# Filling the token slots from two tiles with dump numbers, four tiles for the quarter sums, three tiles for r, a fourth of the squares on ScalarE

## The chip, the cores and the metric

One core of a Trainium2 chip runs the whole program in one launch. The metric is device time in microseconds (us), the median of three runs; lower is better. The engines are TensorE (PE, with its weight loads as PEld), VectorE (DVE), ScalarE (ACT), GpSimd (POOL) and SyncE (SP). Transfers are issued from two queues here, SP's (hardware descriptors, q1 in the views) and POOL's (software descriptors, q0), and are carried by the same 16 DMA engines.

## The reference

```python
scores = matmul(z, z.T) / S                  # 4 batches, S = 3072, z has 64 columns
out = matmul(maximum(scores, 0) ** 2, v)     # v: 3072 x 256
x = (u * out).reshape(12288, 256)

e_idx = argmax(x @ w_gate)                   # 8 experts, top one
for e in range(8):
    h = maximum(x[mask] @ w1[e], 0)          # 256 -> 1024 -> 256
    y[mask] = gate * eom * (h @ w2[e])

h = maximum(y @ w_in, 0)                     # 256 -> 1024, halves u and v
v_n = layer norm of v
v_s = einsum('ts,bsd->btd', w_spatial, v_n) + b_spatial
result = (u * v_s) @ w_out
```

## The kernel before

Every product is made of three matmuls of high and low parts (float32r), so each operand is split into `hi` on ACT and `lo` on DVE. PE, ACT, DVE and SP run in the order in which the code issues; POOL's order is chosen by the framework's scheduler, from what each instruction waits for.

The program has four stages: attention with routing (0 to about 1120 us), the experts (to about 1760), the hidden layer and the norm (to about 2120), and the spatial product, made with two levels of Strassen sums.

**Attention** runs over 576 steps: 4 batches b, 6 column blocks j of 512, 24 row blocks k of 128. For every fourth step PE makes the scores of four steps (L270, 12 matmuls); each step then has `relu` (L218, ACT, tile `r`), `hi` = square of r (L276, ACT), `a` = the same square in full precision (L279 on ACT where `i % 3 == 1`, else L281 on DVE), `lo = a - hi` (L283, DVE), and six matmuls with v (`pv`, L228 to L230), four steps later. `r` has four tiles, shared by all steps. A **group** below is four steps.

Three queues of generators are pumped in the loop. `back` holds the preparation of z and v (load on SP, splits on ACT and DVE, three raw tiles). `fore` holds `route`: after each j it takes 512 tokens through the gates and issues four indirect DMAs on POOL (L429) that scatter their rows, with token number and gate, to a slot in `x_slots`. `slow` holds `first_sums`: 36 times it loads two tiles `sw` of the spatial weight on SP (L788), makes four sums on DVE (L792, L794, L797, L800) and stores each from POOL (L793, L795, L798, L801) to `w_parts`. `sw` has two tiles, and a group of sums uses both, so the next load on SP waits for the stores; whatever SP has behind it (u, z, v loads) waits as well.

The slots must hold something where no token lands. `fill_slots` writes zeros to them in three parts of eight transfers, from one tile of 290 columns that is read again and again (L159), and the parts are queued at steps 22, 46 and 70; each part and each scatter write `x_slots` and wait for each other. `route` drains the current part before it scatters.

**Experts**: `moe_x` loads and turns a chunk of slots and makes, with four small DVE operations (L598 to L601), the row to which each slot's result goes: the token, or for an empty slot a dump row of its own, computed from the tables `marks` and the expert's fill count.

Of the kernel before, what the change touches and what calls it, by code (L numbers as in the profile page):

```python
# [27 lines left out]
F32 = mybir.dt.float32  # L28
F32R = mybir.dt.float32r
BF16 = mybir.dt.bfloat16  # L30
I32 = mybir.dt.int32
AF = mybir.ActivationFunctionType
ALU = mybir.AluOpType
AX = mybir.AxisListType

P = 128
B, S, D, DQK = 4, 3072, 256, 64
N = B * S
E, F = 8, 1024
# [17 lines left out]
class _Kernel:  # L57
# [58 lines left out]
    def setup(self):  # L116
        self.low = [self.below.tile([P, 1024], F32R, name=f"G{i}") for i in range(16)]
        self.G = deque(self.low[0:12])
        self.Z = deque(self.kept[0:6] + self.low[12:])
        self.Z.extend(self.big.tile([P, 1024], F32R, name=f"Z{i}") for i in range(2))  # L120
        nc, wk = self.nc, self.wk
        self.tri = self.pe.tile([P, P], BF16, name="tri", bufs=1)
        make_upper_triangular(nc, self.tri, val=1.0, diag=False)
        self.ones = self.pe.tile([P, P], BF16, name="ones", bufs=1)
        nc.gpsimd.memset(self.ones, 1.0)
        self.WG = self.pe.tile([P, 2, XD], F32R, name="WG", bufs=1)
        self.desc = wk.tile([P, E], F32, name="desc", bufs=1)
        self.base = wk.tile([P, 5, E], F32, name="base", bufs=1)
        for e in range(E):
            nc.gpsimd.memset(self.desc[:, e : e + 1], float(E - e))  # L130
            nc.gpsimd.memset(self.base[:, 0, e : e + 1], float(e * REG))
        self.zeros = self.big.tile([P, W], F32, name="zeros", bufs=1)
        nc.gpsimd.memset(self.zeros, 0.0)
        marks = wk.tile([P, 2, E, CAP // P], I32, name="marks", bufs=1)
        for r0, nt in self.CHUNKS:
            for n, (first, step) in enumerate(((0, REG), (N, CAP))):
                part = marks[:, n, :, r0 : r0 + nt]
                nc.gpsimd.iota(part, pattern=[[step, E], [1, nt]], base=first + r0 * P, channel_multiplier=nt)
        self.marks = wk.tile([P, 2, E, CAP // P], F32, name="marksf", bufs=1)
        nc.vector.tensor_copy(self.marks, marks)  # L140
        self.tokid = wk.tile([P, NT], I32, name="tokid", bufs=1)
        nc.gpsimd.iota(self.tokid, pattern=[[P, NT]], base=0, channel_multiplier=1)

# [7 lines left out]
            nc.vector.tensor_copy(g[:, 0:16], wraw[:, c])  # L151
            nc.vector.tensor_tensor(g[:, 16:32], wraw[:, c], _f(g[:, 0:16]), op=ALU.subtract)

    def fill_slots(self, q):
        r0 = 4 * q
        nt = 4 if q < 2 else CAP // P - r0
        for e in range(E):
            dst = self.xs[e * REG + r0 * P : e * REG + (r0 + nt) * P, :].rearrange("(p r) d -> p r d", p=P)
            self.nc.gpsimd.dma_start(dst, self.zeros.unsqueeze(1).to_broadcast([P, nt, W]))  # L159
            yield  # L160

    def z_prep(self, b, c, dst):
        nc = self.nc
# [33 lines left out]
    def attention(self):  # L197
# [8 lines left out]
        self.drain(deque([zg[0], vg[0]]))  # L206
        self.gate_weights()
        self.back.extend([vg[1], zg[1], vg[2], vg[3], zg[2], vg[4], vg[5]])
        fill = self.fill = deque()

        LAG = 4
        score = [*bank[0:3], bank[7]]
# [1 line left out]
        hl, rs, uts = {}, {}, {}  # L214

        def relu(i):
            rs[i] = self.big.tile([P, 512], F32, name="r", bufs=4)
            nc.scalar.activation(rs[i], score[i % 4], AF.Relu, scale=1.0 / S)  # L218

        def pv(i):  # L220
# [26 lines left out]
        for i, (b, j, k) in enumerate(steps):  # L247
            if i == 0:
                load_u(0)
            if i == NK:  # L250
                self.slow.append(self.first_sums())
            if k == 8:
                load_u(i // NK + 1)
            if k == 0:
                if j == 2 and b + 1 < B:
                    self.back.extend([self.z_prep(b + 1, c, z[b + 1]) for c in range(3)])
                if j == 2 and b == B - 1:
                    self.w0 = []
                    self.back.append(self.w_prep(0, self.w0))
            if k % 4 == 0:  # L260
                self.until(z[b], j // 2)
                self.until(z[b], k // 8)
                (QH, QL), (KH, KL) = z[b][j // 2], z[b][k // 8]
                cs = slice((j % 2) * 512, (j % 2) * 512 + 512)
                for m in (0, 2):
                    for n, (w, x) in enumerate(((KH, QH), (KL, QH), (KH, QL))):
                        for t in range(2):
                            ck = slice((k % 8 + m + t) * P, (k % 8 + m + t) * P + P)
                            rows = slice(64 * t, 64 * t + 64)
                            nc.tensor.matmul(score[m + t], w[rows, ck], x[rows, cs], start=(n == 0), stop=(n == 2))  # L270
                relu(i)
            if k % 4 < 3:
                relu(i + 1)
            r = rs.pop(i)
            hi = self.pe.tile([P, 512], F32R, name="hi", tag="t2h", bufs=6)
            nc.scalar.activation(hi, r, AF.Square)  # L276
            a = self.big.tile([P, 512], F32, name="a", bufs=3)
            if i % 3 == 1:
                nc.scalar.activation(a, r, AF.Square)  # L279
            else:  # L280
                nc.vector.tensor_tensor(a, r, r, op=ALU.mult)  # L281
            lo = self.pe.tile([P, 512], F32R, name="lo", tag="t2l", bufs=5)
            nc.vector.tensor_tensor(lo, a, _f(hi), op=ALU.subtract)  # L283
            hl[i] = (hi, lo)
            if i >= LAG:
                pv(i - LAG)
            self.pump(self.fore)
            if b == B - 1 and j == NJ - 1:
                self.pump(self.fore)
                if k == 12:  # L290
                    self.first_chunk()
            self.pump(self.back)
            if i < NK:
                self.pump(self.back)
            if i < 3 * NK and k == 22:
                fill.append(self.fill_slots(i // NK))
            if i % 2 == 0:
                self.pump(fill)
            if i >= NK and i % 2 == 0 and (j in (1, 3, 4) or b and (j == 0 and k >= 8 or j == 2 and (k >= 12 or b == B - 1))):
                self.pump(self.slow)  # L300
            if j == NJ - 1 and k == NK - 1:
                for t in z.pop(b).values():
                    self.Z.extend(t)
# [6 lines left out]
    def first_chunk(self):  # L310
        nc = self.nc
        self.drain(self.fore)
        self.early = self.wk.tile([P, 1], F32, name="early", bufs=1)
        nc.vector.tensor_copy(self.early, self.base[:, 0, 0:1])
        nc.vector.tensor_scalar(self.base[:, 0, 0:1], self.base[:, 0, 0:1], 1024.0, None, op0=ALU.max)
        self.rows0 = {c: self.moe_load(0, c * 512, 4) for c in range(2)}
        self.x0 = []
        held = [self.G.popleft() for _ in range(2)]
        self.low = [t for t in self.low if all(t is not h for h in held)] + held

        def later():
            for _ in range(13):
                yield
            yield from self.moe_x(self.rows0.pop(0), 0, 0, 4, self.x0, self.early, held, self.bank[3:5])

        self.fore.append(later())

    def route(self, b, j, acc, ut):
# [93 lines left out]
        tt(rk, rk, oh, op=ALU.mult)  # L422
        sl = m4("sl")
        red(sl, rk, AX.X, ALU.add)
        self.drain(self.fill)
        slot = m4("slot", I32)
        nc.vector.tensor_copy(slot, sl)
        for i in range(4):
# [135 lines left out]
        self.nc.sync.dma_start(rows[:, 0:nt, :], src.rearrange("(p r) d -> p r d", p=P))  # L564
        return rows

    def moe_x(self, rows, e, r0, nt, dst, end=None, into=None, T=None):
        nc, wk = self.nc, self.wk
        end = self.base[:, 0, e : e + 1] if end is None else end
        xh, xl = into or (self.e4(F32R), self.e4(F32R))  # L570
        n = nt * P
        T = T or self.bank[6:8]
# [20 lines left out]
        low(1)  # L593
        ids = wk.tile([P, 4], I32, name="ids", bufs=3)
        gate = wk.tile([P, 4], F32, name="gate", bufs=3)
        own, spare = (self.marks[:, k, e, r0 // P : r0 // P + nt] for k in range(2))
        t = wk.tile([P, 4], F32, name="idt", bufs=2)[:, 0:nt]
        nc.vector.tensor_copy(t, rows.bitcast(I32)[:, 0:nt, ID])  # L598
        nc.vector.tensor_tensor(t, t, spare, op=ALU.subtract)
        nc.vector.scalar_tensor_tensor(t, own, end, t, op0=ALU.is_lt, op1=ALU.mult)  # L600
        nc.vector.tensor_tensor(ids[:, 0:nt], t, spare, op=ALU.add)  # L601
        nc.vector.tensor_copy(gate[:, 0:nt], rows[:, 0:nt, ID + 1])
        dst.append((xh, xl, ids, gate))

# [66 lines left out]
    def moe(self):  # L671
# [41 lines left out]
        for i, (c, f) in enumerate(seq):  # L713
# [13 lines left out]
                    self.slow.append(self.gmlp_weights())  # L727
            if f == 3 and c + 1 < len(chunks):
                xx[c + 1] = []
                self.fore.append(self.moe_x(rows.pop(c + 1), *chunks[c + 1], xx[c + 1], self.early if c == 0 else None))  # L730
            if c == 0 and f == 7:
                self.drain(self.fore)
            if f == (5 if c else 7) and c + 2 < len(chunks):
# [47 lines left out]
    def first_sums(self):  # L781

        nc, tt = self.nc, self.nc.vector.tensor_tensor
        for n, (r, c) in self.QUARTER.items():
            for tb, k in [(tb, k) for tb in range(2) for k in range(6)]:
                g = [self.big.tile([P, 768], F32, name="sw", bufs=2) for _ in range(2)]
                for th in range(2):
                    nc.sync.dma_start(g[th].rearrange("p (s t) -> p s t", s=2), self.wsq[r, c, 2 * th + tb, k])  # L788
                yield
# [621 lines left out]
```

## Time and profile before

| | |
|---|---|
| median of three runs | 3420.19 us (3416.14 to 3421.24) |
| profiled execution | 3423.64 us |
| its span, first to last instruction | 3421.8 us |
| PE busy | 3361.7 us |
| DVE busy | 2606.0 us |
| ACT busy | 1678.8 us |
| POOL busy | 717.5 us |

Times in the views are counted from the start of the span. PE is the engine to watch: nearly all its time is matmuls, so a microsecond in which it waits in the first stage is a microsecond of the whole. Busy time of the other engines lies beside it.

### The profile page before, as it was taken

To read this page: it belongs to the slowest core of one execution; us is meant where nothing else is said; L and a number is where in the kernel's file an instruction comes from. 1 tells how busy PE (TensorE), PEld (TensorE's weight loads), DVE (VectorE), ACT (ScalarE), POOL (GpSimd) and SP (SyncE) were. 2 spreads that over 40 slices of the span, in tenths; PEclk is the share of its full clock that TensorE was granted. 3 is DMA by queue.
4 is the path that set the end of the run, shared out by engine and by line. 5 is a ranking of instruction groups with operands and counts; after the bars stand their busy time and mean duration, and the time that the engine had idled before them with its cause. 6 is when DMAs were issued, how large, how long until landed. Compare 5 with 4: busy or idle time off the path is not lost.

```text
span 3421.8 us, 51102 instructions
## 1 busy us (share of the span) xinstructions
PE 3361.7 (98%) x18192; PEld 2970.3 (87%) x18192; DVE 2606.0 (76%) x4803; ACT 1678.8 (49%) x3142; POOL 717.5 (21%) x1037
## 2 busy tenths in 40 slices
PE   7989999999999999999999999999999999999999
PEld 5767777777777888888888889999999999999999
DVE  6768788787887688977768887576767777777777
ACT  6757767677767433333334453333333343343432
POOL 1211121221121356665543320000000000100000
PEclk9999999999999999999999999999999999999999
DMA  5453332323340477777748887576767586975854
GB/s 146 143 149 96 101 115 87 108 96 105 106 137 30 151 263 267 270 275 266 247 156 292 299 317 270 186 263 225 274 219 272 188 282 208 263 264 190 285 195 164
DMA packets 269292, 681.73 MB, mean 199 GB/s; under 512 B 30128, under 2 KB 117952, under 8 KB 269024
## 3 DMA queue, kind: packets, MB, share of 16 engines
q1 hardware_dynamic: 186144, 409.89, 36.5%
q0 software_dynamic: 82880, 268.46, 22.4%
q8 instruction: 144, 2.36, 0.3%
q14 instruction: 124, 1.02, 0.1%
HBM read 429.38 MB, written 248.85 MB: 198 GB/s over the span
## 4 chain that ended last, share of the span: by engine, by line
PE 86%; DVE 5%; DMA 4%; issue 3%; POOL 1%; ACT 1%; DVEq 0%; SPq 0%; POOLq 0%; ACTq 0%
PE bank L1209 11%; PE bank L1208 11%; PE bank L1210 11%; PE bank L228 8%; PE bank L229 7%; PE bank L230 7%; PE bank L270 6%; PE bank L690 4%; PE bank L751 2%; PE bank L752 2%; PE bank L753 2%; PE bank L691 2%; PE bank L975 1%; PE bank L974 1%; PE bank L973 1%
## 5 line engine op out<-in xcount | busy, mean ns | idle before, releaser
L283 DVE TENSOR_TENSOR lo<-a,hi 128x512 fp32r<-128x512 f32 x576 | 394.5, 691 | 156.4 <-ACT a L279 93.0
L218 ACT ACTIVATE r<-bank 128x512 f32<-128x512 f32 x576 | 330.1, 599 | 299.9 <-PE bank L270 272.6
L228 PE MATMUL bank<-hi,G 128*128 128x512 f32 x1152 | 469.1, 407 | 0.0
L229 PE MATMUL bank<-lo,G 128*128 128x512 f32 x1152 | 452.3, 393 | 10.6 <-DVE lo L283 10.6
L1322 ACT ACTIVATE wh<-raw 128x768 fp32r<-128x768 f32 x294 | 247.9, 845 | 417.0 <-PE bank L1210 320.7
L230 PE MATMUL bank<-hi,G 128*128 128x512 f32 x1152 | 450.2, 391 | 0.0
L1208 PE MATMUL bank<-wh,R 128*128 128x384 f32 x1288 | 430.3, 334 | 0.7 <-ACT os L1100 0.7
L1209 PE MATMUL bank<-wl,R 128*128 128x384 f32 x1288 | 430.3, 334 | 0.1
L1210 PE MATMUL bank<-wh,R 128*128 128x384 f32 x1288 | 430.2, 334 | 0.0
L1323 DVE TENSOR_TENSOR wl<-raw,wh 128x768 fp32r<-128x768 f32 x294 | 280.4, 954 | 195.3 <-ACT wh L1322 194.6
L276 ACT ACTIVATE hi<-r 128x512 fp32r<-128x512 f32 x576 | 361.0, 640 | 0.0
L1208 PE MATMUL bank<-wh,K 128*128 128x384 f32 x1064 | 356.8, 335 | 3.9 <-ACT os L1100 3.9
L1209 PE MATMUL bank<-wl,K 128*128 128x384 f32 x1064 | 356.5, 335 | 0.0
L1210 PE MATMUL bank<-wh,K 128*128 128x384 f32 x1064 | 356.4, 335 | 0.0
L755 ACT ACTIVATE hh<-bank 128x512 fp32r<-128x512 f32 (+2 forms) x256 | 132.8, 519 | 386.7 <-PE bank L753 341.6
L228 PEld LDWEIGHTS bank<-hi,G 128*128 128x128 f32 x1152 | 217.4, 189 | 92.0 <-issue 52.0
L281 DVE TENSOR_TENSOR a<-r 128x512 f32<-128x512 f32 x384 | 262.4, 683 | 31.4 <-ACT r L218 30.4
L690 PE MATMUL bank<-G,hh 128*128 128x512 f32 x728 | 263.7, 395 | 0.0
L229 PEld LDWEIGHTS bank<-lo,G 128*128 128x128 f32 x1152 | 218.0, 189 | 50.0 <-DVE lo L283 11.4
L230 PEld LDWEIGHTS bank<-hi,G 128*128 128x128 f32 x1152 | 217.6, 189 | 47.1
L1208 PEld LDWEIGHTS bank<-wh,R 128*128 128x128 f32 x1288 | 241.8, 188 | 1.1 <-ACT os L1100 1.0
L1209 PEld LDWEIGHTS bank<-wl,R 128*128 128x128 f32 x1288 | 241.8, 188 | 0.5 <-DVE wl L1323 0.4
(279 smaller groups left out, 7388.3 us busy)
## 6 DMA issues: line engine op xcount, KB each, us to landing
raw<-w_parts SPq DMA_DIRECT2D x240, 384.0 KB
ra<-v_ops SPq DMA_DIRECT2D x147, 512.0 KB
v_ops<-vu POOLq DMA_DIRECT2D x84, 512.0 KB
xi<-partial SPq DMA_DIRECT2D x48, 768.0 KB
sw<-wsq SPq DMA_DIRECT2D x72, 384.0 KB
w_parts<-sw POOLq DMA_DIRECT2D x144, 192.0 KB
u_hid<-vu POOLq DMA_DIRECT2D x48, 512.0 KB
us<-u_hid SPq DMA_DIRECT2D x31, 768.0 KB
```

The source lines that it names most:

```text
L218: nc.scalar.activation(rs[i], score[i % 4], AF.Relu, scale=1.0 / S)
L228: nc.tensor.matmul(acc[d], vh[:, c], hi, start=(k == 0), stop=False)
L229: nc.tensor.matmul(acc[d], vh[:, c], lo, start=False, stop=False)
L230: nc.tensor.matmul(acc[d], vl[:, c], hi, start=False, stop=(k == NK - 1))
L276: nc.scalar.activation(hi, r, AF.Square)
L281: nc.vector.tensor_tensor(a, r, r, op=ALU.mult)
L283: nc.vector.tensor_tensor(lo, a, _f(hi), op=ALU.subtract)
L690: nc.tensor.matmul(acc, hh[:, tc_], w, start=(f == 0), stop=False)
L1208: nc.tensor.matmul(ps, vh, wh[:, ws], start=(k == 0), stop=False)
L1209: nc.tensor.matmul(ps, vh, wl[:, ws], start=False, stop=False)
L1210: nc.tensor.matmul(ps, vl, wh[:, ws], start=False, stop=(k == 5))
L1323: tt(lo, raw, _f(hi), op=ALU.subtract)
```

## The change

- `fill_slots` is one generator of 32 transfers. It has two tiles `fz` of four rows of 290 columns, cleared once; before each transfer an iota on POOL writes the dump numbers of that chunk into the ID column of one of them, and the transfer copies that tile. The generator stands first in `slow` and is pumped twice a step in the first 24 steps.
- An empty slot then carries its dump row's number, so `moe_x` only converts the ID column; `marks`, `zeros`, `early` and three of its small operations go.
- `first_sums` has four tiles `sw`; it is no longer pumped in the first half of j = 2 of the last batch.
- `r` has three tiles, in the `work` pool under the tag `t2r`, which `f64_prep` uses later.
- `a` is squared on ACT where `i % 4 == 1` (144 of 576 steps; 192 before).

```diff
-        self.zeros = self.big.tile([P, W], F32, name="zeros", bufs=1)
-        nc.gpsimd.memset(self.zeros, 0.0)
...
-    def fill_slots(self, q):
-        r0 = 4 * q
-        nt = 4 if q < 2 else CAP // P - r0
+    def fill_slots(self):
+        nc = self.nc
+        fz = [self.big.tile([P, 4, W], F32, name=f"fz{i}") for i in range(2)]
+        for t in fz:
+            nc.gpsimd.memset(t, 0.0)
+        i = 0
         for e in range(E):
-            dst = self.xs[e * REG + r0 * P : e * REG + (r0 + nt) * P, :].rearrange("(p r) d -> p r d", p=P)
-            self.nc.gpsimd.dma_start(dst, self.zeros.unsqueeze(1).to_broadcast([P, nt, W]))
-            yield
+            for r0, nt in self.CHUNKS:
+                t = fz[i % 2][:, 0:nt, :]
+                i += 1
+                nc.gpsimd.iota(t.bitcast(I32)[:, :, ID], pattern=[[1, nt]], base=N + e * CAP + r0 * P, channel_multiplier=nt)
+                dst = self.xs[e * REG + r0 * P : e * REG + (r0 + nt) * P, :]
+                nc.gpsimd.dma_start(dst.rearrange("(p r) d -> p r d", p=P), t)
+                yield
...
-        fill = self.fill = deque()
+        self.slow.append(self.fill_slots())
...
-            rs[i] = self.big.tile([P, 512], F32, name="r", bufs=4)
+            rs[i] = wk.tile([P, 512], F32, name="r", tag="t2r", bufs=3)
...
-            if i % 3 == 1:
+            if i % 4 == 1:
                 nc.scalar.activation(a, r, AF.Square)
...
-            if i < 3 * NK and k == 22:
-                fill.append(self.fill_slots(i // NK))
-            if i % 2 == 0:
-                self.pump(fill)
-            if i >= NK and i % 2 == 0 and (j in (1, 3, 4) or b and (j == 0 and k >= 8 or j == 2 and (k >= 12 or b == B - 1))):
+                self.pump(self.slow)
+                self.pump(self.slow)
+            elif i % 2 == 0 and (j in (1, 3, 4) or b and (j == 0 and k >= 8 or j == 2 and k >= 12)):
                 self.pump(self.slow)
...
-        self.drain(self.fill)
...
-        own, spare = (self.marks[:, k, e, r0 // P : r0 // P + nt] for k in range(2))
-        t = wk.tile([P, 4], F32, name="idt", bufs=2)[:, 0:nt]
-        nc.vector.tensor_copy(t, rows.bitcast(I32)[:, 0:nt, ID])
-        nc.vector.tensor_tensor(t, t, spare, op=ALU.subtract)
-        nc.vector.scalar_tensor_tensor(t, own, end, t, op0=ALU.is_lt, op1=ALU.mult)
-        nc.vector.tensor_tensor(ids[:, 0:nt], t, spare, op=ALU.add)
+        nc.vector.tensor_copy(ids[:, 0:nt], rows.bitcast(I32)[:, 0:nt, ID])
...
-                g = [self.big.tile([P, 768], F32, name="sw", bufs=2) for _ in range(2)]
+                g = [self.big.tile([P, 768], F32, name="sw", bufs=4) for _ in range(2)]
```

Where the instructions stand now. On POOL at the program's start, before (wraw holds the gate weights):

```order
L133 MEMSET zeros 128x290
L138 IOTA marks 128x8x4 x4
L138 IOTA marks 128x8x3 x2
L138 IOTA marks 128x8x2 x2
L142 IOTA tokid 128x96
L147 DMA wraw<-wg 128x2x16
L159 DMA x_slots<-zeros 512x1x290 x8
L675 IOTA lim 128x4
L793 DMA w_parts<-sw 128x384
```

And of the change, at the same place:

```order
L133 IOTA tokid 128x96
L138 DMA wraw<-wg 128x2x16
L149 MEMSET fz_211 128x1160
L149 MEMSET fz_212 128x1160
L155 IOTA fz_211 128x4
L662 IOTA lim 128x4
L155 IOTA fz_212 128x4
L157 DMA x_slots<-fz_211 128x1160
L157 DMA x_slots<-fz_212 128x1160
L155 IOTA fz_211 128x3
L157 DMA x_slots<-fz_211 128x870
```

Eight transfers in a row, which wait for no buffer, have become two; every later one stands behind an iota that waits until its tile's last transfer has landed. This goes on for 32 transfers, with two stores of sums just ahead of the last; then come the stores of the sums.

On POOL around the second scatter (the second of the program's 24), before:

```order
L429 DMA x_slots<-rows,slot 99328x290 x4
L159 DMA x_slots<-zeros 640x1x290 x2
L793 DMA w_parts<-sw 128x384
L795 DMA w_parts<-sw 128x384
L159 DMA x_slots<-zeros 640x1x290
L798 DMA w_parts<-sw 128x384
L159 DMA x_slots<-zeros 640x1x290 x2
L801 DMA w_parts<-sw 128x384
L159 DMA x_slots<-zeros 640x1x290 x3
```

And of the change (its first row is the first and the second scatter):

```order
L422 DMA x_slots<-rows,slot 99328x290 x8
L780 DMA w_parts<-sw 128x384
L782 DMA w_parts<-sw 128x384
L785 DMA w_parts<-sw 128x384
L788 DMA w_parts<-sw 128x384
```

The fills that stood among the stores of the third group of sums, and those between the two scatters, have left.

On ACT, one group during the same `route` (e is xh of the tokens), before:

```order
L218 ACTIVATE r<-bank_66 128x512
L218 ACTIVATE r<-bank_67 128x512
L276 ACTIVATE hi<-r 128x512
L279 ACTIVATE a<-r 128x512
L218 ACTIVATE r<-bank_68 128x512
L276 ACTIVATE hi<-r 128x512
L340 ACTIVATE e_1738<-e_1737 128x512
L218 ACTIVATE r<-bank_73 128x512
```

And of the change:

```order
L216 ACTIVATE r<-bank_66 128x512
L216 ACTIVATE r<-bank_67 128x512
L274 ACTIVATE hi<-r 128x512
L216 ACTIVATE r<-bank_68 128x512
L274 ACTIVATE hi<-r 128x512
L277 ACTIVATE a<-r 128x512
L334 ACTIVATE e_1774<-e_1773 128x512
L216 ACTIVATE r<-bank_73 128x512
```

The square on ACT has moved from a group's first step to its second, where it stands in every group now; before, its place went round. PE's order has not changed at all, and SP's only in that two of the last loads of `sw` stand behind one more load of u.

## Rows read from the trace of the kernel before

**Rows 1.** The page: busy time, share of the span and instructions of each engine.
```profile
PE 3361.7 (98%) x18192; PEld 2970.3 (87%) x18192; DVE 2606.0 (76%) x4803; ACT 1678.8 (49%) x3142; POOL 717.5 (21%) x1037
```

**Rows 2.** Waits of PE, 36 to 1118 us: us in total, times, longest.
```profile
PE bank L229 <- DVE lo L283: 10.6, 2, 10.1
```

**Rows 3.** Chain that ended last, 0 to 1400 us: start, us, what.
```profile
104.97 1.58 PE bank L270 x12
...
150.36 1.58 PE bank L270 x12
...
253.49 1.58 PE bank L270 x12
...
436.58 1.58 PE bank L270 x12
...
709.77 1.58 PE bank L270 x12
...
987.07 1.58 PE bank L270 x12
```

**Rows 4.** The same chain, 156 to 200 us.
```profile
161.03 2.86 DMA x_slots<-rows,slot
...
170.02 15.24 DMA w_parts<-sw
```

**Rows 5.** Timelines of DVE and ACT near 195, 955 and 410 us; idle before in brackets.
```profile
194.79 0.56 DVE L792 TENSOR_TENSOR sw<-sw 128x384 f32<-128x384 f32 x1 [16.87 <-DMA sw<-wsq]
...
955.23 0.56 DVE L792 TENSOR_TENSOR sw<-sw 128x384 f32<-128x384 f32 x1 [5.01 <-DMA sw<-wsq]
...
410.40 0.63 ACT L180 ACTIVATE K<-raw 128x512 fp32r<-128x512 f32 x1 [3.15 <-DMA raw<-z]
```

**Rows 6.** Waits of SP's queue, 0 to 420 us.
```profile
SPq L788 <- DMA w_parts<-sw: 233.7, 29, 49.6
```

**Rows 7.** Timeline of all engines, 0 to 45 us, and of POOL near 111.
```profile
4.71 5.23 POOL L159 DMA_DIRECT2D x_slots<-zeros  x7
...
26.83 0.63 ACT L180 ACTIVATE G<-raw 128x512 fp32r<-128x512 f32 x1 [8.12 <-DMA raw<-v]
...
28.00 2.13 PE L270 MATMUL bank<-K,K 64*128 64x512 f32 x6 [6.02 <-ACT r L218]
...
34.32 1.15 ACT L180 ACTIVATE G<-raw 128x512 fp32r<-128x512 f32 x2 [3.32 <-DMA raw<-v]
...
36.00 1.64 PE L270 MATMUL bank<-K,K 64*128 64x512 f32 x5 [4.68 <-ACT r L218]
...
110.90 1.46 POOL L429 DMA_INDIRECT x_slots<-rows,slot  x1 [3.54 <-ACT hi L276]
```

**Rows 8.** DMA queues, 10 to 28 us, 34 to 43, 10 to 43: packets, MB, share.
```profile
q0 software_dynamic: 985, 4.07, 81.9%
q1 hardware_dynamic: 899, 1.24, 24.4%
...
q1 hardware_dynamic: 1529, 2.24, 71.2%
...
q1 hardware_dynamic: 2969, 4.43, 43.4%
```

**Rows 9.** Groups of instructions by line, 0 to 1500 us.
```profile
L283 DVE TENSOR_TENSOR lo<-a,hi 128x512 fp32r<-128x512 f32 x576 | 394.5, 691 | 156.4 <-ACT a L279 93.0 <-ACT hi L276 17.2 <-issue 1.5
...
L218 ACT ACTIVATE r<-bank 128x512 f32<-128x512 f32 x576 | 330.1, 599 | 299.9 <-PE bank L270 272.6 <-issue 15.7 <-DVE a L281 11.6
L281 DVE TENSOR_TENSOR a<-r 128x512 f32<-128x512 f32 x384 | 262.4, 683 | 31.4 <-ACT r L218 30.4 <-issue 1.0
```

**Rows 10.** Busy time by windows: us, then PE, PEld, DVE, ACT, POOL, clock, DMA.
```profile
571.24:616.63 45.39, 45.39 (x236) 34.75 (x235) 38.68 (x82) 35.79 (x74) 7.47 (x8) 1.00 0.22 72
```

**Rows 11.** Groups of DVE, 1118 to 1810 us; waits of PE, 1118 to 1300.
```profile
L600 DVE SCALAR_TENSOR_TENSOR idt<-marksf,base,idt 128x4 f32<-128x4 f32 x14 | 3.1, 223 | 0.5
...
PE bank L751 <- DVE hlo L757: 4.0, 5, 1.6
```

More of the change, by code (lines that the diff above doesn't have):

```diff
@@ L131, in setup @@
             nc.gpsimd.memset(self.base[:, 0, e : e + 1], float(e * REG))
-        self.zeros = self.big.tile([P, W], F32, name="zeros", bufs=1)
-        nc.gpsimd.memset(self.zeros, 0.0)
[L134 to L140, printed above, removed]
         self.tokid = wk.tile([P, NT], I32, name="tokid", bufs=1)
@@ L312, in first_chunk @@
         self.drain(self.fore)
-        self.early = self.wk.tile([P, 1], F32, name="early", bufs=1)
-        nc.vector.tensor_copy(self.early, self.base[:, 0, 0:1])
         nc.vector.tensor_scalar(self.base[:, 0, 0:1], self.base[:, 0, 0:1], 1024.0, None, op0=ALU.max)
@@ L323, in later @@
                 yield
-            yield from self.moe_x(self.rows0.pop(0), 0, 0, 4, self.x0, self.early, held, self.bank[3:5])
+            yield from self.moe_x(self.rows0.pop(0), 4, self.x0, held, self.bank[3:5])
         self.fore.append(later())
@@ L565, in moe_load, with moe_x @@
         return rows
-    def moe_x(self, rows, e, r0, nt, dst, end=None, into=None, T=None):
+    def moe_x(self, rows, nt, dst, into=None, T=None):
         nc, wk = self.nc, self.wk
-        end = self.base[:, 0, e : e + 1] if end is None else end
         xh, xl = into or (self.e4(F32R), self.e4(F32R))
@@ L729, in moe @@
                 xx[c + 1] = []
-                self.fore.append(self.moe_x(rows.pop(c + 1), *chunks[c + 1], xx[c + 1], self.early if c == 0 else None))
+                self.fore.append(self.moe_x(rows.pop(c + 1), chunks[c + 1][2], xx[c + 1]))
             if c == 0 and f == 7:
```

## The prediction

> **What bounds the kernel now.** The page's busy times come first: PE is busy for 3361.7 of 3421.8 us, DVE for 2606.0 [rows 1]. Nothing that moves work among ACT, DVE and POOL can pay by itself; only PE's gaps can. So next the waits of PE in the first stage: 10.6 us for `lo`, of which 10.1 in one wait [rows 2]; few and long. A gap costs more than the wait shows, since matmuls run slower for a while after it, so I measured the gaps on the chain instead. The start of the scores of a group is one of its steps, and a block of 24 steps repeats the same pattern: from 104.97 to 150.36 is one block, 45.39 us [rows 3]. Whatever a stretch takes beyond whole blocks is lost:
>
> - 150.36 to 253.49: 103.13, two blocks are 90.78, lost **12.35**;
> - 253.49 to 436.58: 183.09, four are 181.56, lost **1.53**;
> - 436.58 to 709.77: 273.19, six are 272.34, lost **0.85**;
> - 709.77 to 987.07: 277.30, six are 272.34, lost **4.96**.
>
> Together 19.7 us. Everything between runs at PE's own pace.
>
> Then who is late. In the first gap the chain runs through a scatter (2.86) and the store of a sum that took 15.24 [rows 4], then through the load behind it; DVE stands 16.87 us in front of the sum L792, and all its `lo` behind that [rows 5]. The store is slow because five and more fills stand ahead of it in POOL's queue. The load waits for the store because both `sw` tiles are in use; SP waited 233.7 us in 29 such waits in 420 us [rows 6]. The same wait without fills gives the gap at 955 (DVE idle 5.01 before L792), and at 410 it shows as a z load that SP could not issue: ACT stood 3.15 us for it, with `relu` behind [rows 5]. The smaller loss before 709.77 I put down to the same.
>
> Last the start: PE is in steady work only from 36.00. ACT waited 8.12 us for a v tile at 26.83 and 3.32 for the next at 34.32; PE waited 6.02 and 4.68 for the `relu` behind them [rows 7]. From 10 to 28 us the fills carried 4.07 MB and the loads 1.24, which is 226 and 69 GB/s [rows 8].
>
> **The change, part by part.**
>
> *Four `sw` tiles, no fills in the middle.* The load of a group of sums now waits for the stores of the group before the last, which were issued some 18 us or more earlier (a group takes five pumps, every second step, so ten steps of 45.39/24 = 1.89 us). SP stops blocking; z and v loads go out when their raw tile is free. The fills have left the second and third scatter. So the 19.7 us go. Bounds: 12.35 if the other three gaps have another cause that stays, 19.7 if all go. I take 19.
>
> *The start.* Eight fills that wait for nothing become two at a time. One fill is now on average 13 x 128 x 290 x 4 bytes x 8 experts / 32 = 0.48 MB, 2.1 us at 226 GB/s. Its turn round a tile: an issue of 5.23/7 = 0.75 us [rows 7], a completion of about what a small scatter takes, 2.86 [rows 4], the iota (0.25 as an estimate, a third of the issue, since it writes four columns at most), and the transfer: about 6 us for two fills, so 160 GB/s, and the queue holds packets for about 4.3 of 6 us, 71%. While it does, loads get 69 GB/s; else what they reached alone, 2.24 MB in 9 us at a share of 71.2%, or 350 GB/s at full share [rows 8]. That makes 0.71 x 69 + 0.29 x 350 = 150 GB/s, an estimate. From 10 us until the last v tile the loads have 3.6 MB to bring (4.43 by 43 us [rows 8], less the first two of `sw`, 128 x 768 x 4 bytes each, 0.79): 24 us, so it lands at 34 where it came by 43. PE can't use all of that: its first matmuls keep it busy until 28.00 - 6.02 = 22 us, and the place of 36.00 is one round of scores later, at 25 at the earliest. Gain between 0 and 11; I take **6**, as the loads behind that place still share the engines with fills, where they had them alone. All 32 fills take some 16 x 6 = 96 us this way and end just ahead of the first scatter, at 110.90 [rows 7]; should they end 15 us later, nobody waits but that scatter, whose row tile is wanted two blocks on.
>
> The views agree with a rule of the Trainium skill here that speaks against the change: "DMA: Bandwidth & Descriptors", section "Queues, rings and completion order", says that a DMA engine takes turns between queues packet by packet. In [rows 8] 985 packets of the fills stood beside 899 of the loads, 4.1 against 1.4 KB each, which is such a turn. By it alone, with the fills' queue never empty, loads would stay at their 69 GB/s until all fills are out; that is the second rival below.
>
> *r in three tiles.* `relu` of a step waits until `a` of three steps earlier is done, four before. ACT waited 11.6 us for that in 576 steps, hidden behind 272.6 us of its waits for PE [rows 9]. Three steps are 5.7 us and DVE makes `a` right after `r`; its backlog would have to pass 3 us before ACT feels it and some 5 before PE does. I take 0; the bound is the third rival.
>
> *Squares.* 48 squares of 683 ns go to DVE [rows 9]: 33 us over 1090, so in the fullest block DVE goes from 38.68 to 40.05 of 45.39 [rows 10]. It also loses waits: 93.0 us for `a` on ACT fall on 192 steps [rows 9], most of it where the square is a group's first, behind ACT's wait for the scores; now there are 144, all in second place. Net 0, from 1 lost to 1 gained; PE has four steps of slack to both.
>
> *Experts.* Three operations of 0.16 to 0.22 us [rows 11] go from each of 32 chunks, 17 us of DVE. PE waited for `hlo` 4.0 us in the first 180 us [rows 11]; I count nothing for the rest. Gain 0 to 4, I take **1**.
>
> *Sum.* 3423.6 of the profiled execution less 19 + 6 + 1 = 26 gives 3397.6. That execution is 3.4 over the median of the runs shown, so against the median I forecast **3394**.
>
> **Rivals.**
>
> 1. *Only the first gap goes.* POOL's stores still stand behind scatters, which wait for routing, and SP's loads of z could be late for that reason with four tiles too. Against it: the store that held things at 955 is now two groups away. Gain 12.35 + 0 to 3: 3405 to 3408.
> 2. *The fills starve the loads.* 15.4 MB in place of 4.75 pass during the first blocks, and by the packet rule loads get 69 GB/s or less whenever the queue is full. If a landed fill were replaced as fast as its neighbour drains (2.1 us), 3.6 MB take 52 us, and the last v tile comes at 62 where it came by 43: 19 us lost against 20 gained, 3419. The kernel is slower by over 0.2% from 27 us lost on, which is 3.6 MB in 60 us or 60 GB/s; at 50 GB/s it is 72 us, 39 lost, and 3420 - 20 + 39 = 3439. Against it: a turn of 0.75 + 2.86 us is longer than 2.1, so the queue must run dry.
> 3. *DVE becomes the bound.* With 40 of 45.4 us busy, each wait in order costs; if `relu` stalled by 0.35 us in each of 144 groups, 50 us: 3450. Against it: [rows 10] shows PE without a gap in the fullest block. It decides from 0.14 us a group.
>
> The gap at 160 us is the fills' own doing, so that the change would do nothing at all has no mechanism that I see.
>
> **How the numbers follow.** Forecast (all gaps, start 0 to 11): 3385 to 3403, chance 0.65. Rival 1, or a start that gains nothing: 3400 to 3411, 0.20. Rival 2 to no change: 0.07; to slower: 0.04. Rival 3: 0.04. A change within 0.2% (6.8 us) can't be told from none. So faster 0.86, same 0.08, slower 0.06. The range leaves out rivals 2 and 3 and a little below the forecast: 3381 to 3412.
>
> **What would show it.** Right: on the chain, all blocks of the first stage take 45.4 us, no wait of DVE for `sw`, SP's wait for `w_parts` near zero, PE's place of 36.00 at 25 to 33. ACT's wait for `a` may double without a gap of PE. Wrong: PE waiting for `relu` behind v tiles after 30 us (rival 2), a chain that still passes a load of z or `sw` near 400 or 950 us (rival 1), or many small waits of PE for `lo` or `r` spread over the blocks (rival 3).

## The result and the profile after

The median went from 3420.0 to 3382.4 us (3378.4 to 3386.9, four runs of each): a ratio of 0.9891 (95% interval 0.9876 to 0.9905). The sign and the range were right, but the gain was 37.6 us where the prediction summed 26: 3382.4 lies just below its forecast of 3385 to 3403 and 1.4 us inside its range. The profiled execution took 3378.41 us.

The page after, its span and the busy times (engine, us, share, instructions), beside [rows 1]:

```profile
span 3376.6 us, 51132 instructions
PE 3347.1 (99%) x18192; PEld 2963.2 (88%) x18192; DVE 2624.3 (78%) x4753; ACT 1654.5 (49%) x3094; POOL 717.7 (21%) x1070
```

PE executes as many matmuls as before. DVE is busier and PE still done sooner: of the span, PE lost 30.6 us of idle time and 14.6 us in which it was busy. The waits of PE after, 36 to 1080 us (us in total, times, longest), where [rows 2] had 10.6 for `lo` among others:

```profile
PE bank L349 <- DVE e L339: 0.3, 1, 0.3
```

That row is the whole answer of the view. Then the chain, 0 to 1400 us, the places that answer to [rows 3]:

```profile
21.70 1.59 PE bank L268 x11
28.95 1.59 PE bank L268 x12
...
88.82 1.58 PE bank L268 x12
...
134.21 1.58 PE bank L268 x12
...
1042.08 1.58 PE bank L268 x12
```

From 88.82 to 1042.08 are 953.26 us, and 21 blocks of 45.39 are 953.19: nothing is lost between. The place at 88.82 is the one that stood at 104.97, so the start alone gave 16.15. It is seen in PE's rows of scores of a group (idle time ahead of a row would stand in brackets behind it; there is none). Before, behind those of [rows 7]:

```profile
45.02 1.66 PE L270 MATMUL bank<-K,K 64*128 64x512 f32 x12
52.27 1.66 PE L270 MATMUL bank<-K,K 64*128 64x512 f32 x12
```

and after:

```profile
21.63 1.66 PE L268 MATMUL bank<-K,K 64*128 64x512 f32 x12
28.88 1.66 PE L268 MATMUL bank<-K,K 64*128 64x512 f32 x12
```

The place that stood at 36.00 stands at 21.63, 14.4 us earlier. From there to the next scores it took 9.02 us before and takes 7.25 now, 1.8 less, though 7 of the group's 12 score matmuls were already done at 36.00 (29 matmuls fall into the window before, 38 into the one after). The windows of exactly these groups show why (us, then PE, PEld, DVE, ACT and POOL busy, granted clock, DMA share, GB/s); before:

```profile
28.00:36.00 8.00, 2.92 (x7) 1.40 (x7) 3.79 (x7) 4.68 (x10) 0.00 (x0) 0.50 1.01 259
36.00:45.02 9.02, 9.02 (x29) 6.57 (x29) 8.54 (x15) 9.02 (x18) 0.00 (x0) 0.70 0.51 175
45.02:52.27 7.25, 7.25 (x37) 5.48 (x36) 5.92 (x10) 4.80 (x10) 0.00 (x0) 1.00 0.00 1
```

and after:

```profile
21.63:28.88 7.25, 7.25 (x38) 5.49 (x38) 6.85 (x12) 7.25 (x15) 1.50 (x5) 1.00 0.99 361
```

In the eight us in which PE was busy for 2.92, the granted clock was 0.50, that is 1.2 GHz; the group behind them ran at a mean of 0.70. After the change there is no such stretch just ahead, and the same group runs at 1.00.

The v tiles behind it come earlier. ACT's timeline after, where [rows 7] had idle times of 8.12 and 3.32 for v, and POOL's, first fills, last fill and first scatter:

```profile
16.35 0.63 ACT L178 ACTIVATE G<-raw 128x512 fp32r<-128x512 f32 x1 [0.87 <-DMA raw<-v]
...
5.82 1.11 POOL L157 DMA_DIRECT2D x_slots<-fz  x2 [0.15 <-POOL fz L155]
...
13.58 0.13 POOL L155 IOTA fz<- 128x3 int32 x1 [6.65 <-DMA x_slots<-fz]
...
81.72 0.55 POOL L157 DMA_DIRECT2D x_slots<-fz  x1
...
94.56 1.24 POOL L422 DMA_INDIRECT x_slots<-rows,slot  x1 [4.38 <-ACT hi L274]
```

The row at 13.58 is the pacing: POOL writes the next dump numbers only when its tile's last fill has landed, and waited 6.65 us for that. DMA queues after, 10 to 28 us (packets, MB, share of 16 engines; then issues with KB each and median us to landing), beside the first two rows of [rows 8]:

```profile
q1 hardware_dynamic: 2557, 3.39, 56.4%
q0 software_dynamic: 734, 3.11, 44.1%
...
raw<-v SPq DMA_DIRECT2D x3, 512.0 KB, 5.4
x_slots<-fz POOLq DMA_DIRECT2D x2, 580.0 KB, 6.3
```

In 18 us the loads brought 3.39 MB, 188 GB/s, and the fills 3.11 MB, 173 GB/s.

The rest of the gain, by the timelines of PE in the two profiled executions. From the scores of the fourth group to those of the last one of the stage: 1080.70 us before (45.02 to 1125.72), 1061.60 after (28.88 to 1090.48), 19.1 less. From there to the last matmul of the experts' second layer: 6.0 less. Hidden layer: 1.1 more. Spatial product: 5.1 less, which can't be put down to the change: from its first to its last product the stage took between 1357.0 and 1364.1 us in the profiled executions here, and both ends are versions of the kernel before. Start 16.1 + 19.1 + 6.0 - 1.1 + 5.1 = 45.2, which is 3423.64 - 3378.41.

### The profile page after: what moved, and what is told of

It reads as the page before. It is cut to its first block, busy times and chain, and to the rows that moved or that the text cites. A ratio compares the mean times of both kernels' runs of the same rounds, so it can differ in the third digit from the quotient of the medians.

```text
span 3376.6 us, 51132 instructions
## 1 busy us (share of the span) xinstructions
PE 3347.1 (99%) x18192; PEld 2963.2 (88%) x18192; DVE 2624.3 (78%) x4753; ACT 1654.5 (49%) x3094; POOL 717.7 (21%) x1070
## 4 chain that ended last, share of the span: by engine, by line
PE 90%; DMA 3%; issue 2%; DVE 2%; POOL 1%; ACT 1%; SPq 0%; POOLq 0%; DVEq 0%; ACTq 0%
PE bank L1195 12%; PE bank L1196 12%; PE bank L1197 12%; PE bank L226 9%; PE bank L227 8%; PE bank L228 8%; PE bank L268 7%; PE bank L677 4%; PE bank L738 2%; PE bank L739 2%; PE bank L740 2%; PE bank L678 2%; PE bank L962 1%; PE bank L960 1%; PE bank L961 1%
## 5 line engine op out<-in xcount | busy, mean ns | idle before, releaser
L279 DVE TENSOR_TENSOR a<-r 128x512 f32<-128x512 f32 x432 | 295.7, 684 | 41.0 <-ACT r L216 39.6
L744 DVE SCALAR_TENSOR_TENSOR hlo<-bank,hh 128x512 fp32r<-128x512 f32 (+2 forms) x256 | 150.0, 587 | 126.4 <-ACT hh L742 125.7
```

## The experiments

Theory A is the prediction's: the loads of `sw` waited for stores because both tiles were in use, and the start gains because fills in pairs leave the loads their share. The rival, theory B: the gaps are the fills' own doing, by their bytes and their place in the queue, and the tiles matter little. Where a run tests another term, its expectation names that term's own rivals. Each run had the kernel before on the same chip beside it, which took 3420.0 to 3425.2, so runs of different groups are compared by their ratios. "Between" below is the time from the first scores of the fourth group to those of the last.

**The four tiles alone, in the kernel before.**

```diff
-                g = [self.big.tile([P, 768], F32, name="sw", bufs=2) for _ in range(2)]
+                g = [self.big.tile([P, 768], F32, name="sw", bufs=4) for _ in range(2)]
```

> The kernel before with four tiles for the quarter sums and nothing else; fills stay in three parts. Theory A (the gaps come from the load of sums waiting for the stores of the last group, since both tiles are in use): all four gaps of the first stage go although the fills still run between 165 and 186 us, because the load of the third group of sums no longer waits for a store behind them; the start stays late (place of 36.00 unchanged). About 3420 - 20 = 3400. Theory B (the fills' burst itself makes the first gap, by delaying loads that have to pass beside it): the first gap of 12.35 stays for the most part, only the later three (7.3) go: about 3412.

Measured: 3403.6 against 3425.2, ratio 0.9934 (0.9918 to 0.9951). Waits of PE, 40 to 1080 us, the whole answer; a wait of SP's queue, 0 to 420; and PE's start:

```profile
PE bank L355 <- DVE e L345: 0.3, 1, 0.3
...
SPq L788 <- DMA w_parts<-sw: 97.3, 15, 21.6
...
35.91 1.64 PE L270 MATMUL bank<-K,K 64*128 64x512 f32 x5 [5.59 <-ACT r L218]
```

All four gaps are gone (between: 1061.35), with the fills still in the middle; the start is as late as ever. So all the gaps needed the wait for a free tile, the first one too.

**The new fill alone, in the kernel before.** The generator of 32 paced transfers at the start, in place of the three parts; two `sw` tiles and the old dump rows stay. `r` has three tiles, for room.

```diff
-        fill = self.fill = deque()
+        self.fill = deque()
+        self.slow.append(self.fill_slots())
...
-            rs[i] = self.big.tile([P, 512], F32, name="r", bufs=4)
+            rs[i] = wk.tile([P, 512], F32, name="r", tag="t2r", bufs=3)
...
-            if i < 3 * NK and k == 22:
-                fill.append(self.fill_slots(i // NK))
-            if i % 2 == 0:
-                self.pump(fill)
+            if i < NK:
+                self.pump(self.slow)
+                self.pump(self.slow)
```

> The kernel before with the new fill alone (two tiles with dump numbers, all 32 transfers at the start); two tiles for the sums and the old arithmetic of dump rows are kept, r has three tiles since four do not fit beside the fill's. Theory A: the start comes about 16 us earlier and the first gap shrinks to a few us, as no fill stands in front of the stores; the three later gaps (1.5, 0.9, 5.0) stay. About 3420 - 16 - 10 = 3394. Theory B: the same. A rival for the start (the gain there is from the shorter setup on GpSimd, not from the fills' pace) expects the same start too and is told apart by the unpaced fill.

Measured: 3402.1, ratio 0.9928 (0.9907 to 0.9950). The fourth group's scores came at 30.04 where before had them at 45.02. On the chain the gap of 12.35 is gone; 2.2 us are lost at another place, between 83 and 98 us, where DVE waits 6.30 us for the second load of `sw`, itself behind stores that POOL issued just after the last fill. The later gaps are not gone (the smallest, 0.8 near 660, isn't shown):

```profile
371.85 1.59 PE bank L276 x12
...
419.27 1.59 PE bank L276 x12
...
874.04 1.59 PE bank L276 x12
...
968.85 1.35 PE bank L276 x9
```

The first two stand one block apart and took 47.42, 2.0 too much; the other two are two blocks apart and took 94.81, 4.0 too much, near DVE's wait for a load of `sw`:

```profile
929.67 0.56 DVE L797 TENSOR_TENSOR sw<-sw 128x384 f32<-128x384 f32 x1 [3.96 <-DMA sw<-wsq]
```

So the fills' move cures the start and most of the first gap, and the rest needs something else.

**The change with two `sw` tiles.**

```diff
-                g = [self.big.tile([P, 768], F32, name="sw", bufs=4) for _ in range(2)]
+                g = [self.big.tile([P, 768], F32, name="sw", bufs=2) for _ in range(2)]
```

> The changed kernel with two tiles for the quarter sums again. Theory A: the start's gain stays, the three later gaps come back and some of the first: 3382 + 7 to 10 = 3389 to 3392, with SP waiting over 200 us for stores in the first 420. Theory B: the fills were the cause, four tiles are needless: 3382 to 3385.

Measured: 3389.1, ratio 0.9892 (0.9876 to 0.9909). The time is where theory A put it, but that is no hit: the kernel before took 3425.2 beside it, and the ratio is that of the change (0.9891). The traces tell more. Between is 1063.93, 2.3 more than with four tiles. SP's waits, 0 to 420 us, are those of [rows 6] again:

```profile
SPq L775 <- DMA w_parts<-sw: 255.7, 30, 40.1
```

Yet on the chain only 1.0 and 0.7 us are lost:

```profile
82.70 1.58 PE bank L268 x9
...
98.26 1.59 PE bank L268 x12
...
363.35 1.58 PE bank L268 x12
...
394.01 1.59 PE bank L268 x12
```

The first two stand 15.56 apart, and 14.58 in the change (81.51 and 96.09); the other two 30.66, and 29.93 in the change (361.18 and 391.11). None is lost near 950. The run before this one, which still pumped sums in the first half of j = 2 of the last batch, has that gap; the change doesn't pump there. That makes the dropped pumps the likely reason; no run has them alone. They can't be the reason near 385, where that run lost 2.0 with two tiles too: so early in attention the two differ mainly in the squares (a third on ACT there, a fourth here), and no run has that alone with two tiles. So theory A's three gaps did not come back whole. The edits overlap: the gaps have more than one cure in the change, and the tiles, worth 19 us alone, are worth 2 in this stage beside the others.

**The change with unpaced fills.** The numbers are written once a tile, so that a fill doesn't wait for the last one of its tile; the trace shows eight issued in a row, and each later one behind a landing. Empty slots then share dump rows, which nobody reads.

```diff
+            nc.gpsimd.iota(t.bitcast(I32)[:, :, ID], pattern=[[1, 4]], base=N, channel_multiplier=4)
...
-                nc.gpsimd.iota(t.bitcast(I32)[:, :, ID], pattern=[[1, nt]], base=N + e * CAP + r0 * P, channel_multiplier=nt)
```

> The changed kernel with the dump numbers written once into each of the two tiles (so the slots' numbers repeat; all of them are still rows that nobody reads), so that no fill waits for the one before it and only the framework's eight transfers in flight bound them. Theory A (the start gains because two fills in flight leave the DMA engines to the loads for part of the time): loads get about 69 GB/s beside the fills again and now for longer, the place of 36.00 comes at 36 to 55 instead of 21.7, 3382 + 14 to 33 = 3396 to 3415. Rival (the gain at the start comes from the source rows of 4640 bytes in a row instead of 1160 read four times, or from the shorter setup): no difference, 3382 to 3385.

Measured: 3399.7, ratio 0.9922 (0.9905 to 0.9938), where the change has 0.9891: some 11 us lost. The loss is at the start. PE's timeline to 55 us and the DMA queues, 10 to 43 us:

```profile
30.34 1.65 PE L268 MATMUL bank<-K,K 64*128 64x512 f32 x5 [4.58 <-ACT r L216]
...
46.10 1.64 PE L268 MATMUL bank<-K,K 64*128 64x512 f32 x5 [1.25 <-ACT r L216]
54.42 1.66 PE L268 MATMUL bank<-K,K 64*128 64x512 f32 x12
...
q0 software_dynamic: 2438, 10.51, 77.3%
q1 hardware_dynamic: 2270, 3.14, 25.6%
...
x_slots<-fz POOLq DMA_DIRECT2D x10, 580.0 KB, 11.9
...
raw<-v SPq DMA_DIRECT2D x4, 512.0 KB, 16.1
```

The place of 36.00 came at 30.34, not at 36 to 55 as expected: PE stood one group later, whose last scores came at 46.10. The fifth group's scores came at 54.42; in the change at 36.13, 18.3 earlier, and in before at 52.27. From there to the last scores it is 1054.7 us, and 1054.4 in the change. Unpaced, a v tile takes 16.1 us to land in place of 5.4, and the loads get 95 GB/s. So the gain at the start is the pacing's.

**The old dump-row arithmetic in the change** (`marks`, `early` and the three small operations back).

```diff
-        nc.vector.tensor_copy(ids[:, 0:nt], rows.bitcast(I32)[:, 0:nt, ID])
+        own, spare = (self.marks[:, k, e, r0 // P : r0 // P + nt] for k in range(2))
+        t = wk.tile([P, 4], F32, name="idt", bufs=2)[:, 0:nt]
+        nc.vector.tensor_copy(t, rows.bitcast(I32)[:, 0:nt, ID])
+        nc.vector.tensor_tensor(t, t, spare, op=ALU.subtract)
+        nc.vector.scalar_tensor_tensor(t, own, end, t, op0=ALU.is_lt, op1=ALU.mult)
+        nc.vector.tensor_tensor(ids[:, 0:nt], t, spare, op=ALU.add)
```

> The changed kernel with the old arithmetic of the dump rows put back in the experts stage (tables of marks at the start, three more small VectorE operations for each of 32 chunks); the fill and all else stay. Theory A (the experts gain little from these operations; most of the 6 us that this stage was shorter by in one profiled execution is its spread): 0 to 3 us more than the change, 3382 to 3386. Rival (the 17 us of VectorE work were on the path): 5 to 7 more, 3388.

Measured: 3389.2, ratio 0.9893 (0.9877 to 0.9910). The two versions below with a third of the squares on ACT and with four tiles r took 3382.1 and 3381.6 on the same chip, so this one is 7 us slower, as the rival had it. Waits of PE, 1130 to 1765 us, here, and then in the change:

```profile
PE bank L753 <- DVE hlo L759: 10.8, 13, 2.7
```

```profile
PE bank L738 <- DVE hlo L744: 5.5, 8, 1.5
```

From the last scores to the end of the experts' second layer, four traces with the old arithmetic took 633.8 to 637.8 us, mean 636.1; seven with the new and nothing else changed in this stage took 626.9 to 630.7, mean 629.5. So three operations of 0.2 us in each of 32 chunks were worth 6.5 us, not 1.

**A third of the squares on ACT, or none.** `i % 4 == 1` became `i % 3 == 1` in one run, and never in the other.

```diff
-            if i % 4 == 1:
+            if i % 3 == 1:
```

```diff
-            if i % 4 == 1:
+            if i < 0:
```

> The changed kernel with a third of the squares on ScalarE again. Theory A (PE has slack to both engines): no difference, 3380 to 3385, with VectorE's wait for a back near 90 us. Rival (place of the square in a group matters): a few us more.

> The changed kernel with all squares on VectorE (144 more of 683 ns, 98 us). Theory A: VectorE would need 40.05 + 6 x 0.683 = 44.1 of 45.39 us in the fullest block of attention and about 42 in the others, with hardly a wait left that can't be hidden: 0 to 8 us more than the change, where the blocks with route and sums together show waits of PE for lo. Rival (VectorE is already the bound at its limit): 20 or more.

Measured: 3382.1 with a third, ratio 0.9874 (0.9857 to 0.9890), no difference from the change; 3396.6 with none, 0.9913 (0.9897 to 0.9930). Waits of DVE for ACT's square, 22 to 1080 us, with a third and then with a fourth:

```profile
DVE lo L281 <- ACT a L277: 93.1, 81, 2.1
```

```profile
DVE lo L281 <- ACT a L277: 39.0, 64, 1.3
```

and the waits of PE with none:

```profile
PE bank L349 <- DVE e L339: 9.3, 12, 1.7
PE bank L227 <- DVE lo L281: 0.7, 1, 0.7
```

From a third to a fourth DVE's waits more than halved and PE doesn't feel it: they are slack. With none on ACT, between is 1075.33, 13.7 more, which falls between the two theories (0 to 8, or 20 and more). Of the blocks from 52 us on 12 of 22 have a gap, of 0.5 to 2.5 us, all behind 279 us; in them PE waits for `e`, which DVE makes in `route`, and DVE is busy for 43.4 of 47.0 us in the first of them. Rival 3 of the prediction is real, but one quarter of the squares away.

**Four tiles for r in the change.**

```diff
-            rs[i] = wk.tile([P, 512], F32, name="r", tag="t2r", bufs=3)
+            rs[i] = wk.tile([P, 512], F32, name="r", tag="t2r", bufs=4)
...
```

The other tiles under the tag `t2r` have four with it.

> The changed kernel with four tiles under the tag that r now uses. Theory A: no difference (3380 to 3385), ScalarE's wait for a drops but it was hidden. Rival: three tiles cost ScalarE, and PE behind it, some us: 3378 or less.

Measured: 3381.6, ratio 0.9874 (0.9858 to 0.9891). No difference: three tiles were enough.

**Can more be had in the experts?** The change was run again beside three versions: the two small copies that are left per chunk moved to ACT, three tiles `so` for the other group of weight sums, and both.

```diff
-        nc.vector.tensor_copy(ids[:, 0:nt], rows.bitcast(I32)[:, 0:nt, ID])
-        nc.vector.tensor_copy(gate[:, 0:nt], rows[:, 0:nt, ID + 1])
+        nc.scalar.copy(ids[:, 0:nt], rows.bitcast(I32)[:, 0:nt, ID])
+        nc.scalar.copy(gate[:, 0:nt], rows[:, 0:nt, ID + 1])
...
-                o = wk.tile([P, 768], F32, name="so", bufs=2)
+                o = wk.tile([P, 768], F32, name="so", bufs=3)
```

> The changed kernel as it is, once more, for its spread and to stand beside the other kernels of this call on one chip. 0.988 to 0.990 of before; between 3378 and 3387, with the spread in the last stage (spatial product), where two executions so far differ by 5 us in loads of the right-hand operand.

> The changed kernel with the two small copies that are left for each chunk (row numbers and gates) on ScalarE, which is busy for under 40% of the experts stage. Theory A (in the experts every small VectorE operation is partly on the path: three of 0.16 to 0.22 us in 32 chunks cost 6 us, so two of 0.16 cost about 3 to 4): 2 to 4 us less than the change. Rival (ScalarE's queue passes the delay on to relu of the next chunk): no difference or 1 to 3 us more.

> The changed kernel with three tiles in place of two for the second level of sums in the experts stage. Theory A: VectorE's waits there for stores of sums (4.6 us in three before) shrink, 1 to 3 us less than the change. Rival: they fall beside VectorE's wait for ScalarE: no difference.

> The changed kernel with both: 3 to 6 us less than the change if both theories hold.

Measured, against 3425.2: again 3384.1, 0.9879 (0.9863 to 0.9896); copies 3382.4, 0.9881 (0.9865 to 0.9898); three tiles 3382.2, 0.9875 (0.9858 to 0.9891); both 3379.8, 0.9868 (0.9851 to 0.9884). Both has the lowest median of all, but its interval overlaps the change's. Waits of PE, 1130 to 1765 us, with the copies on ACT:

```profile
PE bank L738 <- DVE hlo L744: 5.1, 7, 1.4
PE bank L888 <- ACTq L613: 3.1, 1, 3.1
```

5.1 for 5.5, and from the last scores to the end of the second layer 628.4 us where the change run again has 628.9 (three tiles 628.8, both 627.5): the expectation of 2 to 4 us less, that each small operation on DVE counts alike, has fallen.

## Why the prediction was right, and where it was not

- **Gaps: 19 taken, 19.1 to 19.7 measured.** Mechanism and price held: all four gaps needed one wait, as the four tiles alone showed. What the prediction didn't see is that the other edits cure most of it too, so the terms of parts don't add up from runs of single edits. That the first gap is the fills' own doing is half true: with four tiles they stood in the same place and cost PE nothing.
- **"SP stops blocking": wrong.** I looked for a wait of SP for `w_parts` near zero. It stayed for half of the loads and got shorter, and another grew, for DVE's product with u, which frees the tile of the next u load. Before (the first is in [rows 6]) and then after, 0 to 420 us:

```profile
SPq L244 <- DVE e L338: 83.4, 7, 40.8
```

```profile
SPq L242 <- DVE e L332: 227.5, 8, 43.4
SPq L775 <- DMA w_parts<-sw: 108.5, 15, 21.7
```

All of SP's waits together are 384.6 us before and 385.8 after. SP was blocked as long as ever, only no engine stood still for what was behind it. The sign to look for was DVE's wait for `sw`; before, 0 to 1120 us, it was the row below, and after there is none.

```profile
DVE sw L792 <- DMA sw<-wsq: 21.9, 2, 16.9
```

- **Start: 6 taken, bounds 0 to 11, 16.1 measured.** This is the term that was mis-sized. Loads got 188 GB/s where the estimate was 150, and the bound was wrong in two places: the place of 36.00 can follow the first matmuls at once, at 21.6, without the round of scores that I put between; and the slow matmuls behind a gap, 1.8 us, which I had named for the other gaps, were left out. In the run of the change again the fourth group's scores came at 30.62 in place of 28.88, so some 2 us of the 16.1 vary. The fills got 173 GB/s where 160 was estimated; the last was issued at 81.7, within the 96, and the first scatter waited for none of them.
- **Experts: 1 taken, bounds 0 to 4, 6.0 to 6.5 measured.** The second mis-sized term. I counted PE's wait in 180 us and nothing after. Over the whole stage, from the last scores on, PE's waits for `hlo` went from 7.8 to 5.5 us, its idle time from 9.9 to 6.6 and its busy time, for the same 3491 matmuls, from 625.1 to 622.4: the named waits show the loss only in part. DVE was busy 496.7 of 634.9 us before and 481.1 of 629.0 after, so it had time to spare in both. Why three operations cost 6.5 us and the two copies left cost nothing is open; the three depended on each other and the copies don't, but no run tested that.
- **r and squares: 0 and 0, right, but r for a reason that I had misread.** The 11.6 us that ACT waited for `a` [rows 9] were not spread over 576 steps: they are one wait, in the first gap, at 196.58. Told as "may double", ACT's wait for `a` is 0.8 us in the change. DVE's waits for ACT's square are 39.0.
- **Rivals.** 1 fell with the four tiles alone. 2 is a true mechanism: unpaced, it took the start 18.3 us later than paced, 2.2 later than before. What kept it away was what I had argued: a tile's turn, with its wait for the landing, is longer than its drain. 3 would need a quarter of the squares more on DVE. The Trainium skill ("DMA: Bandwidth & Descriptors", section "Queues, rings and completion order") says that a DMA engine takes turns between queues packet by packet. The unpaced run agrees: 2438 packets of fills stood beside 2270 of loads, with 4.3 and 1.4 KB to a packet.
- **Against the sum:** 19.1 + 16.1 + 6.0 are 41 of profiled executions; the medians differ by 37.6. The profiled execution of before was 3.6 above its median, that of the change 4.0 below, and the change's own four runs spread by 8.5.

## What to carry to other kernels

A queue in order makes a wait for a buffer a wait of all that stands behind it. Long waits of the queue prove nothing by themselves: look at which engine is late behind one, and give that buffer the tiles that take it out of the way before making anything faster. Background transfers that share the DMA engines with loads should be paced by a dependency of their own (two tiles rewritten in turn), because the pace decides what the loads get: the same fills left them 188 GB/s paced and 86 unpaced (10 to 28 us). And when one run undoes one edit, a small loss says only that another edit covers it; the edit alone in the old kernel tells the rest.

## What the runs showed of the hardware

- Unpaced fills from contiguous rows of four slots (4640 bytes) moved 5.91 MB from 10 to 28 us in 79.6% of the engines' time; the fills of before, which read one slot's row again and again, moved 4.07 MB in 81.9% [rows 8], beside loads in both. What part the rows have in it was not tried alone.
- With more fills in flight each took longer: 580 KB landed in 6.3 us with two under way beside loads (10 to 28 us), in 11.9 unpaced (10 to 43 us).
- The granted clock stayed at 0.50 in a stretch where PE was busy 2.92 of 8.00 us, and what was left of the group behind it took 9.02 us where the whole group takes 7.25: this gap cost more than its idle time.
